# Delta-rule attention and an MLP on one core: a token group's key transposes are issued one unit earlier, and the last two output tiles leave with one DMA per queue instead of two

## The chip, the cores and the metric

One core of a Trainium2 chip runs the whole program. The metric is the device time of one execution in microseconds. Three runs of the kernel before took 662.1, 662.82 and 663.01 us; the median is 662.82 us.

## The reference

Two stages follow each other. The first is a delta-rule recurrence over 768 time steps for 4 batches and 8 heads of width 48. The second is an MLP with a hard-swish over 3072 tokens, with 384 inputs, 2048 hidden units and 384 outputs.

```python
q, k, v: (4, 8, 768, 48)   beta: (4, 8, 768)   w_in: (384, 2048)   w_out: (2048, 384)
k_n = k / (norm(k) + 1e-6);  state = 0                    # (B, H, 48, 48)
for t in range(768):
    y[t]   = q[t] @ state
    state += beta[t] * outer(k_n[t], v[t] - k_n[t] @ state)
x = y.transpose(0, 2, 1, 3).reshape(4 * 768, 8 * 48)      # row b*768 + s
h = x @ w_in
out = (h * clip(h + 3, 0, 6) / 6) @ w_out                 # (3072, 384), float32
```

A row of `out` is one token; the 768 tokens of a batch lie behind one another, so the same time steps of two batches lie 768 rows apart.

## The kernel before

**Tiles.** The 768 steps are cut into N = 24 chunks `t` of C = 32 steps. A chunk of all four batches fills the 128 partitions: batch b has the 32 partitions `rows(b)`. For every chunk there is a preparation, which does not need the state, and a chain, which does. Two chunks make a block (CB = 2) of 256 tokens, and the MLP works block by block: an "up" stage into the hidden units and a "down" stage out of them. There are 12 blocks, 0 to 11.

**Preparation** (`prep`, from L494). Its steps, one per `yield`: POOL normalises the keys into `kb` (L499); TensorE transposes the keys, four 128x128 transposes into a PSUM tile `pt` (L513), and ScalarE copies them to `KQ` (L521), after which POOL makes the mask `mb` (L475); TensorE transposes the queries and ScalarE copies them; TensorE multiplies the two into `sc` (L536); VectorE masks `sc` (L547).

**Chain** (`chain`, from L776). Products with the state `ks` (L795), VectorE combines them with the values to `R` (L890, L898), TensorE applies the inverse, `pz` (L816), ScalarE copies it back to `R` (L916), TensorE updates the state, `su` (L927, added on VectorE at L945), and the output part makes `y` (L832, L808, `py` L816, L852), transposes it, `yt` (L862), and ScalarE writes the transposed tile to the block's `xT` (L866), the MLP's input.

**MLP.** From block 3 on, "up" is `up_by_eleven` (L1055 products, ScalarE L1069, POOL sums L1019, VectorE L1082 and L1086). It multiplies sums of the four tiles of `xT`, which VectorE forms in `token_sums` (L1045) as soon as the block's second `xT` is there. From block 2 on, "down" is `down_by_seven` (L1215 products of 128x192, ScalarE copies L1222, POOL or VectorE adds L1225, VectorE sums L1201). The last adds finish the two output tiles `o[:, 0]` and `o[:, 1]`, and `to_dram` (L1140) stores them.

**What sets the order.** The program is written out by hand. An order string covers the beginning. Then a loop over the chunks (t from LS = 5 to 23) runs NU = 15 units per chunk; in each unit it takes steps of the chain and of the preparations by the table `plan`, then one step of the MLP (`take(units)`). Every engine executes its instructions in the order in which they were issued, so a step's place in `plan` decides what stands ahead of it on TensorE. For t = 6 and later, the preparation taken in `plan` (`now = third`) is that of chunk t + 6, so these steps exist for t = 6 to 17 (chunks 12 to 23). Its first step, `kb`, is taken in unit 13 of the chunk before (`later`). PSUM tiles of the MLP, the transposes, `pz`, `py` and `yt` share four banks (`pm`); a new tile takes the bank whose reader was issued longest ago.

**The output's rows.** `py` is written with the batches exchanged in pairs (`b ^ 1`), so the rows of x, and of `o`, carry batch b in the partitions of batch b ^ 1. `to_dram` undoes that with one DMA of 32 rows per batch. All stores go to SyncE's queue (SP), but for the last block (chunks 22 and 23), where batches 1 and 3 go to ScalarE's queue. In the last block chunk 22's tile leaves in two halves of 192 columns, the first half early; the others at the very end.

Of the kernel before, what the change touches and what calls it, by code (L numbers as in the profile page):

```python
# [14 lines left out]
ACTF = mybir.ActivationFunctionType  # L15
# [29 lines left out]
def kernel(  # L45
# [21 lines left out]
    nc = tc.nc  # L67
    B, H, S, D = q.shape
    DM, FF = moe_w_in.shape
    C, DP = 32, 64  # L70
    P = B * C
    assert P == 128 and S % C == 0 and D <= DP and H % 2 == 0
    N = S // C
# [6 lines left out]
    CB = 2  # L80
# [14 lines left out]
    def rows(b):  # L95
        return slice(C * b, C * b + C)
# [4 lines left out]
    def group(t):  # L101
        return (0, t) if t < G0 else ((t - G0) // GS + 1, (t - G0) % GS)
# [34 lines left out]
    def needs(*what):  # L137
        assert past.issuperset(what), (what, set(what) - past)
# [5 lines left out]
    def ring(tag, n, key):  # L144

        held = rings.setdefault(tag, [])
        i = len(held)
        if i < n:
            held.append(key)
        else:  # L150
            i = min(range(n), key=lambda i: reads.get(held[i], len(reads)))
            needs(("read", held[i]))
            held[i] = key
        slot[tag] = f"{tag}{i}"

    def read(*keys):
        for key in keys:
            past.add(("read", key))
            reads.setdefault(key, len(reads))
# [49 lines left out]
    for j, value in enumerate((1.0, -1.0)):  # L209
        m = mask2[:, j, :]  # L210
        for b in range(B):
            nc.gpsimd.memset(mask2[rows(b), j, :], value)
            nc.gpsimd.affine_select(
                out=mask2[rows(b), j, :], in_=mask2[rows(b), j, :], pattern=[[1, C]],
# [89 lines left out]
    for i, n in enumerate((0, 1, 2, 3, 4, 5, 0, 1, 3, 4, 5, 0, 1, 5, 0, 1)):  # L304
        s, f = weights[i][0].shape[1:]
# [458 lines left out]
    xTs, outs, zs = {}, {}, {}  # L764
# [5 lines left out]
    def he(h):  # L770
        return (h % 2) * NP + h // 2

    def by_pair(t):
        return t.rearrange("p (a e w) -> p e a w", e=2, w=D)

    def chain(t, whole=True):  # L776
# [29 lines left out]
        def plus(out, ph, sign, into):  # L806
            for e in range(2):
                nc.vector.scalar_tensor_tensor(  # L808
                    out=by_pair(out)[:, e], in0=ph[:, e], scalar=sign, in1=by_pair(into)[:, e],
                    op0=ALU.mult, op1=ALU.add,  # L810
                )
# [14 lines left out]
        def output(Z=None):  # L826

            if t > 0:
                needs(("turned", t - 1))
            y = work.tile([P, DM], FP32, name="y", bufs=1)  # L830
            if t > 0:
                nc.scalar.activation(  # L832
                    out=by_pair(y[:]), in_=even, func=ACTF.Copy, scale=parity[:, 1, 1:2]
                )
                past.add(("even", t))
                if ("R", t) in past:
                    read(("ks", t, 0))
                yield 1
                plus(y[:], odd, parity[:, 0, 1:2], y[:])
                read(*(("ks", t, i) for i in range(2)))  # L840
                yield
            needs(("Z", t))
            Z = zs.pop(t)
            ring("pm", NPM, ("py", t))
            py = psM.tile([P, 512], FP32, name="py", tag=slot["pm"])
            of_heads(py, lambda b: b ^ 1, lambda h: LB[:, he(h), :], Z)
            past.add(("BZ", t))
            yield
            if t == 0:
                nc.scalar.activation(out=y[:], in_=py[:, 0:DM], func=ACTF.Copy)  # L850
            else:
                nc.vector.tensor_tensor(out=y[:], in0=y[:], in1=py[:, 0:DM], op=ALU.add)  # L852
            read(("py", t))
            yield
            blk, cc = divmod(t, CB)
            if cc == 0:
                needs(*([("up", blk - 2)] if blk >= 2 else []))
                xTs[blk] = work.tile([128, NKT, TB], FP32, name="xT")
            ring("pm", NPM, ("yt", t))
            pt = psM.tile([128, NKT, P], FP32, name="yt", tag=slot["pm"])  # L860
            for s in range(NKT):
                nc.tensor.transpose(pt[:, s, :], y[:, s * 128 : (s + 1) * 128], ident[:])  # L862
            past.add(("turned", t))
            yield 1
            read(("yt", t))
            nc.scalar.activation(  # L866
                out=xTs[blk][:, :, cc * P : (cc + 1) * P], in_=pt[:], func=ACTF.Copy
            )
            past.add(("seam", t))
            yield  # L870

# [11 lines left out]
        else:  # L883
# [5 lines left out]
            for e in range(2):  # L889
                nc.vector.scalar_tensor_tensor(  # L890
                    out=Rp[:, e].rearrange("p (a w) -> p a w", w=D), in0=even[:, e],
# [4 lines left out]
            if whole:  # L896
                yield
            nc.vector.scalar_tensor_tensor(  # L898
                out=Rp, in0=odd.rearrange("p e a w -> p e (a w)"), scalar=parity[:, 1, 0:1],
# [43 lines left out]
        for i, x in enumerate(su):  # L943
            sv = state[:, 2 * i : 2 * i + 2].rearrange("p b a w -> p b (a w)")
            nc.vector.tensor_tensor(  # L945
                out=sv, in0=sv, in1=x[:, :, 0 : NP * D], op=ALU.subtract
# [187 lines left out]
                yield  # L1134

    def to_dram(t, o, m=slice(0, DM)):
        for b in range(B):
            r0 = b * S + t * C
            eng = nc.scalar if t >= N - CB and b % 2 else nc.sync
            eng.dma_start(out=out[r0 : r0 + C, m], in_=o[rows(b ^ 1), m])  # L1140

    def down(blk, c, f0):

# [186 lines left out]
    def take(gen, n=1):  # L1330
        for _ in range(n):
            while next(gen, None) == 1:
                pass
# [107 lines left out]
    with tc.manual_schedule():  # L1441
        for word in ORDER.split():
            word, _, n = word.partition("*")
            for _ in range(int(n or 1)):
                do(word)
        for name in relus:
            settle(0, name)
        while evicts:
            evicts.pop(0)()

        units = gens["u"]
        fill = inverse_of(2)
        loads = iter(())
        left = due = 0
        USED = {"up": 0.42, "eleven": 1.0, "down": 0.7}
        APART = (8, 12)
        CHAIN = {0: 0.45, 1: 0.75, 2: 0.75, 3: 0.4, 4: 0.4, 6: 0.5, 9: 0.8, 10: 0.6, 14: 0.2}
        for t in range(LS, N):
            g, i = group(t)
            ch = chain_of(t)  # L1460
            behind = t == LS
            now, more, third, later = (prep_of(t + LA - n) for n in (2, 1, 0, -1))
            if not behind:
                now = third
            take(gens["v"], 4)
            if i == 0:
                left += 1
            if i == 2:
                loads = keys_of(g + 3)
            plan = {  # L1470
                0: lambda: take(ch),
                1: lambda: (take(ch), take(now)),
                2: lambda: (take(ch), take(now), take(gens["q"], 4)),
                3: lambda: take(ch),
                4: lambda: (take(ch), take(now, t not in APART)),
                5: lambda: take(now, t not in APART),
                6: lambda: take(now),
                7: lambda: take(now, t in APART),
                8: lambda: take(ch),
                9: lambda: take(ch),  # L1480
                10: lambda: take(ch),
                11: lambda: token_sums(t // CB),
                13: lambda: take(later),
            }
            if behind:
                plan[13] = None
                for u, gen in zip((3, 5, 5, 6, 7, 9, 10, 11, 12, 13), (more,) * 5 + (third,) * 5):
                    plan[u] = lambda old=plan.get(u), gen=gen: (old and old(), take(gen))
            ready = (1, 6)
            for u in range(NU):  # L1490
                if plan.get(u):
                    plan[u]()
                take(loads, 2)
                if (i, u) == (0, 2):
                    drain(fill)
                    left = 0
                    fill = norms_of(g + 2)
                if (i, u) == ready:
                    drain(fill)
                    fill = inverse_of(g + 1)  # L1500
                    take(fill)
                    left, due = 2 * (C - 2) + 2, 0.0
                take(rest)
                take(gens["a"])
                take(units)
                settle(1)
                while evicts:
                    evicts.pop(0)()
                if i == 1 == ready[0] and 5 < u < 7:
                    continue  # L1510
                if i == 0 or not left:
                    take(fill, 2 if i or u < 2 else u > 4)
                    continue
                room = max(1.65 - USED[mode["of"]] - CHAIN.get(u, 0), 0.15) / mode["mean"]
                due += room * left / max((GS - i) * NU - u, 1)
                due = min(due, 2.6)
                take(fill, int(due))
                left, due = max(left - int(due), 0), due - int(due)
            if behind:
                take(later)  # L1520
            drain(ch)
        for _ in units:
            settle(2)
# [30 lines left out]
```

## Time and profile before

| what | value |
|---|---|
| median of three runs | 662.82 us |
| the profiled execution's own time | 662.71 us |
| its span from first to last instruction | 661.0 us |
| TensorE busy, share of the span | 96% |
| weight loads busy | 86% |
| VectorE / ScalarE / POOL busy | 76% / 40% / 34% |
| granted TensorE clock, mean | 0.99 |
| stores of output: 48 KB on SP / 24 KB on SP / 24 KB on ScalarE / 48 KB on ScalarE | 90 / 4 / 4 / 2 |

How to read it: a row of the timeline gives the start and the length in us, the engine, the line, the operation with its tiles and the number of instructions that were merged into the row. The length of a matmul is modelled and runs past the start of the next; what one costs is read from start to start. A float32 product has two records (the 32 products `ks` appear as x64), a transpose one. Engines with a `q` behind their name (SPq, ACTq, POOLq) are the sequencers, which issue DMAs and wait on semaphores. In a row of the windows view stand the stretch and its length, busy time and count of each engine, the clock, the mean busy share of the 16 DMA engines and the rate.

### The profile page before, as it was taken

What the parts mean: (1) busy time and instruction counts of PE and PEld (TensorE: products, weight loads), DVE (VectorE), ACT (ScalarE), POOL (GpSimd) and SP (SyncE); (2) the same over time, 40 slices, a digit from 0 to 9 for tenths busy, and PEclk for the clock granted to TensorE, in tenths of its full rate; (3) what the DMA queues carried; (4) which work ended last, traced back from release to release, by engine and by line L of the source; (5) the groups of instructions that cost most, each with busy time, mean ns of one, the idle gap of its engine ahead of it and who ended that gap; (6) DMA issues with size and microseconds to landing.
All of it is one profiled execution on the core that took longest, in us unless ns stands there. A gap on an engine that the chain in (4) does not pass through costs nothing.

```text
span 661.0 us, 26631 instructions
## 1 busy us (share of the span) xinstructions
PE 632.6 (96%) x11640; PEld 568.8 (86%) x11640; DVE 499.5 (76%) x1164; ACT 263.2 (40%) x547; POOL 226.6 (34%) x352
## 2 busy tenths in 40 slices
PE   2768999999999999999999999999999999999997
PEld 2658987776689989999999999999999999999997
DVE  5899877798657988758988748979658998456354
ACT  4786578322232154154144244244244144153240
POOL 5531023003661354453254354164152241331330
PEclk9979999999999999999999999999999999999999
DMA  7888246212041030041030030030020020000101
GB/s 171 210 216 217 76 100 165 49 25 39 16 84 20 2 75 3 3 83 28 3 74 3 2 74 3 2 63 2 3 50 2 2 49 3 23 18 2 26 1 24
DMA packets 88692, 33.28 MB, mean 50 GB/s; under 512 B 80224, under 2 KB 83424, under 8 KB 88576
## 3 DMA queue, kind: packets, MB, share of 16 engines
q1 hardware_dynamic: 88224, 31.29, 21.5%
q8 instruction: 91, 1.49, 0.9%
q10 hardware_dynamic: 352, 0.30, 0.2%
q14 instruction: 25, 0.20, 0.1%
HBM read 26.84 MB, written 4.72 MB: 48 GB/s over the span
## 4 chain that ended last, share of the span: by engine, by line
PE 91%; DVE 3%; DMA 2%; ACT 2%; SPq 1%; issue 1%; ACTq 0%; DVEq 0%
PE po L1215 28%; PE ph L1055 27%; PE ph L983 9%; PE po L1151 6%; PE ks L795 4%; PE pz L816 3%; PE pt L513 3%; PE py L816 3%; PE su L927 3%; PE sc L536 3%; ACT spare L345 1%; PE yt L862 1%; DMA w_out<-in_moe_w_in_dram 1%; SPq L168 1%; PE pi L673 1%
## 5 line engine op out<-in xcount | busy, mean ns | idle before, releaser
L1055 PE MATMUL ph<-xT,w_in 128*128 128x128 f32 (+1 forms) x720 | 156.7, 321 | 0.2 <-issue 0.2
L1019 POOL TENSOR_TENSOR g<-g 128x256 f32<-128x256 f32 (+1 forms) x144 | 88.0, 612 | 105.5 <-ACT g L1069 99.9
L1055 PEld LDWEIGHTS ph<-xT,w_in 128*128 128x128 f32 x720 | 116.9, 191 | 6.7
L1215 PE MATMUL po<-w_out,g 128*128 128x192 f32 x640 | 110.6, 326 | 0.0
L1215 PEld LDWEIGHTS po<-w_out,g 128*128 128x128 f32 x640 | 104.6, 190 | 0.5
L1215 PE MATMUL po<-spare,g 128*128 128x192 f32 x480 | 86.7, 332 | 0.0
L1069 ACT ACTIVATE g<-ph 128x512 f32<-128x512 f32 x72 | 43.0, 597 | 107.5 <-PE ph L1055 107.5
L1215 PEld LDWEIGHTS po<-spare,g 128*128 128x128 f32 x480 | 77.2, 190 | 1.8
L983 PE MATMUL ph<-xT,w_in 128*128 128x128 f32 (+1 forms) x384 | 72.8, 339 | 1.5 <-ACT xT L866 0.6
L1225 POOL TENSOR_TENSOR o<-o,u 128x192 f32<-128x192 f32 x18 | 14.9, 828 | 163.5 <-ACT o L1222 76.1
L983 PEld LDWEIGHTS ph<-xT,w_in 128*128 128x128 f32 x384 | 60.2, 196 | 9.0 <-DVE g L993 0.9
L1082 DVE TENSOR_TENSOR g<-ph,g 128x256 f32<-128x256 f32 x72 | 30.2, 419 | 47.3 <-PE ph L1055 44.8
L748 DVE TENSOR_TENSOR pr<-A 128x30 f32<-128x30 f32 (+9 forms) x150 | 57.6, 384 | 3.3
L1201 DVE TENSOR_TENSOR g<-g 128x512 f32<-128x512 f32 x80 | 55.3, 712 | 3.6 <-PE po L1215 3.6
L1102 DVE SCALAR_TENSOR_TENSOR g<-o,g 128x512 f32<-128x512 f32 x72 | 52.5, 729 | 7.2 <-ACT o L1099 7.2
L753 DVE TENSOR_TENSOR A<-A,pr 128x30 f32<-128x30 f32 (+9 forms) x150 | 55.1, 367 | 3.3
L1055 PE MATMUL ph<-beta_tok,sums_in 128*128 128x128 f32 x288 | 55.9, 275 | 0.1
L1099 ACT ACTIVATE o<-g 128x512 f32<-128x512 f32 x72 | 45.4, 631 | 12.0 <-DVE g L1102 8.5
L345 ACT ACTIVATE spare<-spare 128x768 uint16<-128x768 uint16 (+1 forms) x56 | 47.3, 850 | 3.2 <-DMA kf<-in_k_dram 1.7
L499 POOL TENSOR_TENSOR kb<-kf,inv 128x384 f32<-128x384 f32 x24 | 21.7, 906 | 75.5 <-issue 42.6
L1222 ACT ACTIVATE o<-po 128x192 f32<-128x192 f32 x40 | 13.2, 330 | 83.2 <-PE po L1215 83.2
L1151 PE MATMUL po<-w_out,g 128*128 128x384 f32 x128 | 45.4, 490 | 0.0
(137 smaller groups left out, 1010.2 us busy)
## 6 DMA issues: line engine op xcount, KB each, us to landing
kf<-in_k_dram SPq DMA_DIRECT2D x96, 48.0 KB, 3.0
qb<-in_q_dram SPq DMA_DIRECT2D x96, 48.0 KB, 2.6
vf<-in_v_dram SPq DMA_DIRECT2D x96, 48.0 KB, 2.5
out_dram<-o SPq DMA_DIRECT2D x90, 48.0 KB, 1.6
spare<-in_moe_w_in_dram SPq DMA_DIRECT2D x4, 768.0 KB, 5.3
w_out<-in_moe_w_in_dram SPq DMA_DIRECT2D x4, 768.0 KB, 5.6
w_out<-in_moe_w_out_dram SPq DMA_DIRECT2D x4, 768.0 KB, 7.0
spare<-in_moe_w_out_dram SPq DMA_DIRECT2D x4, 768.0 KB, 4.9
```

Of the source, the lines that this page charges most:

```text
L345: nc.scalar.activation(out=z, in_=z if n else d.bitcast(I16)[:, :, :, 3], func=func, bias=value, scale=scale,)
L748: nc.vector.tensor_tensor(out=pv, in0=A[:, j + 1 :, j].unsqueeze(2).to_broadcast([n, w, j]), in1=A[:, j, 0:j].unsqueeze(1).to_broadcast([n ...
L753: nc.vector.tensor_tensor(out=A[:, j + 1 :, 0:j], in0=A[:, j + 1 :, 0:j], in1=pv, op=ALU.subtract)
L983: nc.tensor.matmul(ph[:, cols], lhsT=w_in[:, s, f * 128 : (f + 1) * 128], rhs=xT[:, s, cols], start=(s == 0), stop=(s == NKT - 1),)
L1019: nc.gpsimd.tensor_tensor(out=out, in0=a, in1=b, op=op)
L1055: nc.tensor.matmul(ph[:, n], lhsT=w, rhs=x, start=start, stop=stop, skip_group_check=True)
L1069: nc.scalar.activation(out=gt, in_=ph[:], func=ACTF.Copy)
L1099: nc.scalar.activation(out=r, in_=g, func=ACTF.Relu, bias=0.5, scale=1.0 / 6.0)
L1102: nc.vector.scalar_tensor_tensor(out=g, in0=r, scalar=1.0, in1=g, op0=ALU.min, op1=ALU.mult)
L1151: nc.tensor.matmul(pos[c][:], lhsT=gs[blk, f // 2][:, f % 2, c * P : (c + 1) * P], rhs=w_out[:, f, :], start=(f == 0), stop=(f == NFC - 1),)
L1201: nc.vector.tensor_tensor(out=A(f, *out, 4), in0=A(f, *a, 4), in1=A(f, *b, 4), op=op)
L1215: nc.tensor.matmul(ps[n][:], lhsT=A(f - f % 2, *a)[:, f % 2], rhs=b[:, f], start=(f == 0), stop=(f == HF - 1),)
```

## The change

```diff
@@ chain, output part
-            nc.scalar.activation(
-                out=xTs[blk][:, :, cc * P : (cc + 1) * P], in_=pt[:], func=ACTF.Copy
-            )
+            xt = xTs[blk][:, :, cc * P : (cc + 1) * P]
+            if blk + 1 < N // CB:
+                nc.scalar.activation(out=xt, in_=pt[:], func=ACTF.Copy)
+            else:
+                xt, src = (x.rearrange("p s (i j c) -> j p s i c", j=2, c=C) for x in (xt, pt[:]))
+                for j in range(2):
+                    nc.scalar.activation(out=xt[j], in_=src[1 - j], func=ACTF.Copy)
@@ to_dram
+        if t >= N - CB:
+            by_batch = out.rearrange("(b s) m -> b s m", s=S)[:, t * C : (t + 1) * C, m]
+            half = B // 2
+            for i, eng in enumerate((nc.sync, nc.scalar)):
+                eng.dma_start(
+                    out=by_batch[i * half : (i + 1) * half],
+                    in_=o[i * half * C : (i + 1) * half * C, m],
+                )
+            return
         for b in range(B):
             r0 = b * S + t * C
-            eng = nc.scalar if t >= N - CB and b % 2 else nc.sync
-            eng.dma_start(out=out[r0 : r0 + C, m], in_=o[rows(b ^ 1), m])
+            nc.sync.dma_start(out=out[r0 : r0 + C, m], in_=o[rows(b ^ 1), m])
@@ the loop over the chunks
+            if not behind:
+                plan.update({
+                    0: lambda: (take(ch), take(now)),
+                    1: lambda: take(ch),
+                })
```

Three things change. First, for t = 6 to 17 the keys' transposes move from unit 1 to unit 0: on TensorE they stand directly behind the products `ks`, and the MLP's step of unit 0 comes after them. Their copy on ScalarE moves ahead of one MLP copy, and in the blocks with `up_by_eleven` the mask on POOL moves ahead of one pair of sums. Second, in the last block x is written with the batches back in their own places, in two ScalarE operations of 192 elements per partition instead of one of 384. Third, therefore, a tile of the last block is stored with one DMA on each queue: 64 partitions of `o`, read as 64 rows, written to a pattern of 2 batches by 32 rows by 192 or 384 columns. Before, each queue had two DMAs of 32 rows by 32 rows. The last block's three stores make 6 DMAs instead of 12. VectorE's order, and SP's ahead of the last block, stay as they were.

## The prediction

> **What bounds the kernel now.** I read the page first: the busy times and the chain that ended last.
>
> ```profile
> span 661.0 us, 26631 instructions
> ...
> PE 632.6 (96%) x11640; PEld 568.8 (86%) x11640; DVE 499.5 (76%) x1164; ACT 263.2 (40%) x547; POOL 226.6 (34%) x352
> ...
> PE 91%; DVE 3%; DMA 2%; ACT 2%; SPq 1%; issue 1%; ACTq 0%; DVEq 0%
> ```
>
> TensorE holds 91% of the chain. After the start it hardly waits, so time can be won on it only through fewer or cheaper records, and at the end of the program only through what follows its last product. The timeline of the last microseconds and the windows behind it show that part.
>
> ```profile
> 656.87 1.92 SPq L1140 DMA_DIRECT2D out_dram<-o  x4
> 656.87 1.93 ACTq L1140 DMA_DIRECT2D out_dram<-o  x4
> 657.57 0.35 DVE L1225 TENSOR_TENSOR o<-u,po 128x192 f32<-128x192 f32 x1 [0.73 <-PE po L1215]
> ```
>
> ```profile
> 656.80:657.60 0.80, 0.73 (x5) 0.43 (x3) 0.07 (x2) 0.00 (x0) 0.00 (x0) 1.00 0.00 0
> 657.60:657.80 0.20, 0.00 (x0) 0.00 (x0) 0.20 (x1) 0.00 (x0) 0.00 (x0) 1.00 0.40 100
> 657.80:658.60 0.80, 0.00 (x0) 0.00 (x0) 0.12 (x1) 0.00 (x0) 0.00 (x0) 1.00 0.90 213
> 659.20:659.60 0.40, 0.00 (x0) 0.00 (x0) 0.00 (x0) 0.00 (x0) 0.00 (x0) 1.00 0.51 117
> 659.60:659.80 0.20, 0.00 (x0) 0.00 (x0) 0.00 (x0) 0.00 (x0) 0.00 (x0) 1.00 0.05 12
> 659.80:661.00 1.20, 0.00 (x0) 0.00 (x0) 0.00 (x0) 0.00 (x0) 0.00 (x0) 0.59 0.00 0
> ```
>
> The last two columns are the DMA engines' mean busy share and the rate in GB/s. The stores of chunk 23 are issued at 656.87. The first bytes move at about 657.7, 0.8 us later. The last add ends at 657.92 and releases the second half of chunk 22. The last bytes move at about 659.7, and the span ends 1.3 us after them. From 657.92 on nothing but stores is left: every microsecond that they take longer is a microsecond of the result.
>
> **The transposes.** They are moved, not removed; the step issues the four transposes, one ScalarE copy and the mask, and no DMA. Twelve chunks have them (t = 6 to 17). I price them by TensorE's timeline, start to start, first at t = 9 and then at t = 5, where the trace already has transposes directly behind `ks`.
>
> ```profile
> 258.80 1.15 PE L795 MATMUL ks<-state,KQ 64*64 64x48 f32 x64
> 259.88 1.57 PE L1215 MATMUL po<-spare,g 128*128 128x192 f32 x8
> 261.29 0.60 PE L513 MATMUL pt<-ident,kb 128*128 128x128 f32 x4
> 261.72 1.47 PE L1215 MATMUL po<-spare,g 128*128 128x192 f32 x8
> 263.03 0.60 PE L513 MATMUL pt<-ident,qb 128*128 128x128 f32 x4
> ```
>
> ```profile
> 117.75 0.66 PE L513 MATMUL pt<-ident,kb 128*128 128x128 f32 x4
> ...
> 118.24 0.60 PE L513 MATMUL pt<-ident,qb 128*128 128x128 f32 x4
> ...
> 118.68 1.13 PE L1151 MATMUL po<-w_out,g 128*128 128x384 f32 x3
> ```
>
> Eight `po` records cost 1.41 us behind `ks` and 1.31 behind transposes: coming from the small tiles costs them 0.10. Four transposes cost 0.49 behind `ks` and 0.44 behind other transposes: 0.05. Today the 0.10 is paid, afterwards the 0.05, since the MLP then comes behind transposes. That is 12 x 0.05 = 0.6 us won. The `up_by_eleven` chunks pay the same entry:
>
> ```profile
> 234.88 0.49 PE L1055 MATMUL ph<-xT,w_in 128*128 128x128 f32 x2
> 235.21 0.39 PE L1055 MATMUL ph<-beta_tok,sums_in 128*128 128x128 f32 x2
> ...
> 235.88 0.60 PE L513 MATMUL pt<-ident,kb 128*128 128x128 f32 x4
> ```
>
> The first pair takes 0.33, the other three 0.67 together, 0.22 each: 0.11 for the entry. The bounds of the gain are 0 (all entries alike) and 12 x 0.10 = 1.2 us (transposes enter free).
>
> What the moved step needs must be ready about 1.0 to 1.4 us earlier. Its keys are tightest in these chunks:
>
> ```profile
> 233.57 0.98 POOL L499 TENSOR_TENSOR kb<-kf,inv 128x384 f32<-128x384 f32 x1
> ...
> 237.97 1.19 POOL L475 TENSOR_TENSOR mb<-beta_tok,mask 128x256 f32<-128x256 f32 x2
> ```
>
> ```profile
> 241.97 0.41 DVE L1082 TENSOR_TENSOR g<-ph,g 128x256 f32<-128x256 f32 x1
> ```
>
> `kb` ends at 234.55, 0.33 us ahead of the products' end at 234.88, so I cost the wait at nothing; without that cover it is a rival below. The mask, 1.19 us, now stands ahead of the POOL sums of the third product group. They can come later by that much at most; their reader on VectorE runs at 241.97, some 4 us after them. The ScalarE copy `KQ` (0.6 us) goes ahead of one copy whose bank is next needed a unit later. For the transposes' bank, in the odd chunks the one that `po` took at 259.88 goes to them at the same time. Nothing queues behind any of this that TensorE needs sooner.
>
> **x in two operations.**
>
> ```profile
> L866 ACT ACTIVATE xT<-yt 128x384 f32<-128x384 f32 x24 | 11.8, 490 | 46.1 <-PE yt L862 46.0
> L1222 ACT ACTIVATE o<-po 128x192 f32<-128x192 f32 x40 | 13.2, 330 | 83.2 <-PE po L1215 83.2
> ```
>
> ```profile
> 618.87 0.68 DVE L1045 TENSOR_TENSOR xT<-xT 128x128 f32<-128x128 f32 x1
> ...
> 619.46 0.28 DVE L1045 TENSOR_TENSOR beta_tok<-xT,beta_tok 128x128 f32<-128x128 f32 x1
> ...
> 620.14 0.39 PE L1055 MATMUL ph<-xT,w_in 128*128 128x128 f32 x2
> ```
>
> Two ScalarE operations of 192 elements take 0.66 us instead of 0.49: 0.17 later; if each cost as much as the whole, 0.49 later. VectorE's sums follow. The third, ending at 619.55, is needed at 620.14: 0.59 of slack. I take nothing, and above 0.59 the excess would count.
>
> **The stores.** Two DMAs per queue become one, so the second issue of the last pair falls away: 0.36 us, the distance between two issues on SP (363 ns median below). But the shape changes too, and the DMA views show what hangs on it.
>
> ```profile
> L1140 SPq DMA_DIRECT2D out_dram<-o x6: 314/363/479, 647.9 to 658.3; - x6
> ```
>
> ```profile
> DMA packets 576, 0.39 MB, mean 23 GB/s; under 512 B 192, under 2 KB 576, under 8 KB 576
> ```
>
> ```profile
> q10 hardware_dynamic: 64, 0.10, 7.1%
> ...
> spare<-in_beta_dram ACTq DMA_DIRECT2D x4, 24.0 KB
> ```
>
> The first DMA row is of 645 to 662 us: 12 stores of 32 rows. The rows are 768 or 1536 bytes, so the 192 small packets are something else, 16 per store: one completion per DMA engine. The second is of the first 7.5 us: four loads of `beta` on ScalarE's queue, 8 rows of 3072 bytes each. Of their 64 packets 32 are rows, which leaves 8 completions per load. So 32 outer rows ran on 16 engines and 8 outer rows on 8: a DMA is cut along its outermost count. The new stores have 64 outermost in SBUF and **2** outermost in DRAM. All transfers of this trace have the same outer count on both sides, so it does not say which side decides; a cut has to fall in the same place on both, and the smaller count allows 2. The bounds are 2 engines and 16, and I take 2. Whether both queues get the same two is not shown either: 2 or 4 engines together. I take 2, since both queues spread over the same 16 today.
>
> The Trainium skill says the same ("DMA: Bandwidth & Descriptors", section "Why a DMA increments its semaphore by 16 and not by 1"): a DMA runs on the largest number of engines up to 16 that divides the slowest dimension of both sides, which is 2 here, and on these queues on the lowest-numbered ones, so the same two. The 16 and the 8 above agree; no run here shows a 2 yet.
>
> What an engine moves, from the busiest stretch of the loads:
>
> ```profile
> 40.00:41.50 1.50, 1.50 (x9) 1.50 (x8) 1.50 (x4) 1.44 (x3) 0.83 (x1) 0.50 0.99 371
> ```
>
> 371 GB/s over 16 x 0.99 busy engines is 23.4 GB/s for one; in the stores above, 213 over 16 x 0.90 is 14.8, with all engines reading the same 32 partitions at once. Behind the end stand 4 x 48 KB and 4 x 24 KB = 288 KB = 295 kB. Two engines need 295 / 46.8 = 6.3 us, or at 14.8 each 10.0 us. I take 6.3, because two engines crowd each other less than sixteen. The issue of the new form is not shown: nothing more at best, 0.2 at worst (the longest store issue, 479 ns, less 314); I take 0.1. The last bytes then move at 657.7 + 0.1 + 6.3 = 664.1 instead of 659.7: **4.4 us later**. The early half of chunk 22's store, 10 us ahead, is hidden even so.
>
> The Trainium skill's figure of about 27 GiB/s per engine (same page, section "Specifications") would give, as an estimate, 5.1 us instead of 6.3.
>
> **The sum.** The profiled execution took 662.71 us, 0.11 under the median. 662.71 - 0.6 + 4.4 = **666.5 us**, 0.6% slower.
>
> **The rivals.**
> - *The stores keep 16 engines* (SBUF's 64 rows decide). Not slower: the last issue falls away, 662.71 - 0.6 - 0.36 = 661.75. The point of decision: with n engines the bytes end at 657.7 + 12.6 / n, which equals 659.7 + 0.6 at n = 5. For it speaks that 64 rows are there to be cut, against it the 8 of the `beta` loads. Chance 0.10.
> - *Two engines per queue, four in all*: 3.15 us, 657.7 + 0.1 + 3.15 = 660.95, so 662.71 + 1.25 - 0.6 = 663.4. Nothing in the rows speaks for it. Chance 0.05.
> - *Two engines at the crowded rate*: 10.0 us, 662.71 + 8.1 - 0.6 = 670.2. For it speaks that 14.8 is the rate of stores, against it that sixteen shared one group of partitions. Chance 0.20.
> - *The transposes wait for `kb`*: from a lateness of 0.33 us on, in the five `up_by_eleven` chunks. If `kb` began only at the products' end, 0.98 x 5 = 4.9 us on top, 671.4. Against it speaks that POOL's work ahead of `kb` is not changed. Chance 0.03.
>
> **How the numbers follow.** The forecast has 0.62. Its own range comes from the DMA view of 8 to 50 us, 40 slices:
>
> ```profile
> DMA  7699999999999799773799938997457999277999
> GB/s 120 121 390 312 229 310 372 230 124 318 363 161 125 162 362 301 138 127 65 140 394 305 182 74 153 369 301 150 75 89 224 390 237 125 39 111 172 384 326 393
> ```
>
> The fastest slice moves 394 GB/s at a digit of 9, so at most 27 GB/s per engine, 5.4 us; with 1.2 won on the transposes and no longer issue, 662.71 + 3.4 - 1.2 = 664.9. Above, it meets the crowded rate. I give 664.9 to 670.4, which holds the forecast and the third rival. A measurement of this kernel tells about 0.2% (1.3 us) from no change: slower 0.85 (forecast and the last two rivals), the same 0.13, faster 0.02 (the first rival with all 1.2 us won).
>
> **What would show it.** In the changed kernel the DMA share behind 658 us should be near 2/16 = 0.13 for some 6 us, at about 47 GB/s, and the 6 stores should leave 12 small packets instead of 192. TensorE's last product should end 0.6 us earlier, with `pt` 0.49 us behind `ks` and `po` at 1.31 per eight records after it, and no wait on `kb`. If the share behind 658 is again 0.5 to 0.9, the first rival holds and the forecast is wrong.

## The result, and the profile after

The changed kernel took 668.93 us (median of 6 runs, 668.21 to 669.08), beside 662.46 us (660.83 to 665.27) for the kernel before in the same rounds. The ratio is 1.0087, with a 95% interval of 1.0067 to 1.0108: slower by 4.4 to 7.2 us. The forecast was 666.5 us, with a range of 664.9 to 670.4.

The page of the changed kernel, with the span, the busy times and the chain that ended last:

```profile
span 666.9 us, 26608 instructions
...
PE 631.7 (95%) x11640; PEld 568.1 (85%) x11640; DVE 501.7 (75%) x1164; ACT 265.0 (40%) x549; POOL 227.4 (34%) x352
...
PE 91%; DMA 3%; DVE 3%; issue 1%; SPq 1%; ACT 1%; DVEq 0%
```

TensorE's busy time fell by 0.9 us, and yet the span grew by 5.9. The end of the program shows where. First the timeline (start, length, engine, line, operation), then the windows behind it (stretch and length, busy time of PE, PEld, DVE, ACT and POOL, clock, DMA share, GB/s), then the count of packets from the DMA view of 648 to 668 us:

```profile
656.96 1.60 ACTq L1145 DMA_DIRECT2D out_dram<-o  x2
657.66 0.35 DVE L1237 TENSOR_TENSOR o<-u,po 128x192 f32<-128x192 f32 x1 [0.73 <-PE po L1227]
```

```profile
657.60:658.00 0.40, 0.02 (x1) 0.00 (x0) 0.34 (x1) 0.00 (x0) 0.00 (x0) 1.00 0.00 0
658.00:659.40 1.40, 0.00 (x0) 0.00 (x0) 0.01 (x1) 0.00 (x0) 0.00 (x0) 1.00 0.12 16
659.40:662.00 2.60, 0.00 (x0) 0.00 (x0) 0.00 (x0) 0.00 (x0) 0.00 (x0) 1.00 0.13 40
662.00:665.00 3.00, 0.00 (x0) 0.00 (x0) 0.00 (x0) 0.00 (x0) 0.00 (x0) 0.64 0.13 47
665.00:665.60 0.60, 0.00 (x0) 0.00 (x0) 0.00 (x0) 0.00 (x0) 0.00 (x0) 0.50 0.13 42
665.60:666.90 1.30, 0.00 (x0) 0.00 (x0) 0.00 (x0) 0.00 (x0) 0.00 (x0) 0.50 0.00 1
```

```profile
DMA packets 396, 0.39 MB, mean 20 GB/s; under 512 B 12, under 2 KB 396, under 8 KB 396
```

The last add ends at 657.66 + 0.35 = 658.01, and the span goes on to 666.9: 8.9 us with nothing in them but stores, where the kernel before had 3.1 (657.92 to 661.0). The DMA share there is 0.13, which is 2 of 16 engines, all the time, and the six stores leave 12 small packets, 2 each. The share before was up to 0.90, with 16 small packets per store. The rate is 16 GB/s in the first 1.4 us and comes up to 47.

On TensorE the products `ks` of t = 6 and t = 18 frame the twelve chunks in which the transposes moved. Their rows, first of the kernel before, then of the changed one:

```profile
183.17 1.15 PE L795 MATMUL ks<-state,KQ 64*64 64x48 f32 x64
...
484.31 1.15 PE L795 MATMUL ks<-state,KQ 64*64 64x48 f32 x64
```

```profile
184.33 1.15 PE L795 MATMUL ks<-state,KQ 64*64 64x48 f32 x64
...
484.41 1.15 PE L795 MATMUL ks<-state,KQ 64*64 64x48 f32 x64
```

With these rows and the last adds both spans fall into four parts:

| part | before | after | difference | forecast |
|---|---|---|---|---|
| start to `ks` of t = 6 | 183.17 | 184.33 | +1.16 | 0 |
| `ks` of t = 6 to `ks` of t = 18 | 301.14 | 300.08 | -1.06 | -0.6 |
| `ks` of t = 18 to the end of the last add | 173.61 | 173.60 | 0.0 | 0 |
| end of the last add to the end of the span | 3.1 | 8.9 | +5.8 | +4.4 |
| span | 661.0 | 666.9 | +5.9 | +3.8 |

The first part has the same instructions in both kernels. Over these two and the seven other profiled executions below, its end lies anywhere from 180.9 to 186.6 us, so the +1.16 is scatter of single executions. The other three parts agree between executions of the same code within 0.15 us. Together they say +4.8 us, inside the measured 4.4 to 7.2.

### The profile page after: what moved, and what is told of

It reads as the page before. It is cut to its first block, busy times and chain, and to the rows that moved or that the text cites. A ratio compares the mean times of both kernels' runs of the same rounds, so it can differ in the third digit from the quotient of the medians.

```text
span 666.9 us, 26608 instructions
## 1 busy us (share of the span) xinstructions
PE 631.7 (95%) x11640; PEld 568.1 (85%) x11640; DVE 501.7 (75%) x1164; ACT 265.0 (40%) x549; POOL 227.4 (34%) x352
## 4 chain that ended last, share of the span: by engine, by line
PE 91%; DMA 3%; DVE 3%; issue 1%; SPq 1%; ACT 1%; DVEq 0%
PE po L1227 28%; PE ph L1059 27%; PE ph L987 9%; PE po L1163 6%; PE ks L795 4%; PE pt L513 4%; PE su L931 3%; PE pz L816 3%; PE py L816 3%; PE sc L536 3%; PE yt L862 1%; DMA w_out<-in_moe_w_in_dram 1%; PE pi L673 1%; DMA spare<-in_moe_w_in_dram 1%; DMA qb<-in_q_dram 1%
## 5 line engine op out<-in xcount | busy, mean ns | idle before, releaser
L1227 PE MATMUL po<-spare,g 128*128 128x192 f32 x480 | 85.1, 331 | 0.0
L1237 POOL TENSOR_TENSOR o<-o,u 128x192 f32<-128x192 f32 x18 | 13.4, 744 | 163.2 <-ACT o L1234 75.5
```

What stands on the lines that cost most here:

```text
L1227: nc.tensor.matmul(ps[n][:], lhsT=A(f - f % 2, *a)[:, f % 2], rhs=b[:, f], start=(f == 0), stop=(f == HF - 1),)
```

## The experiments

The theory is that of the prediction: the time went to the six new stores, because the 2 that stands outermost in their DRAM pattern lets each use two DMA engines, and the move of the transposes gives back a little. The rivals to be told apart from it: the two-level pattern, or the smaller number of DMAs, is slow by itself however many engines there are; and the transposes or the split of x cost something that the tail hides. The first four of them (stores of 32 rows to four engines) were timed beside a kernel before of 663.05 us (median, 29 runs), the last three beside one of 661.52 us (17 runs); the last two have a single run and are read from their traces. The small packets in the table are the completions, one per engine and store.

| kernel | ratio to before, 95% interval | `ks` t = 6 to t = 18 | last add to end | small packets |
|---|---|---|---|---|
| before | 1 | 301.14 | 3.1 | 192 |
| changed | 1.0087 (1.0067 to 1.0108) | 300.08 | 8.9 | 12 |
| stores of 32 rows | 0.9993 (0.9979 to 1.0007) | 300.10 | 3.1 | 192 |
| stores alone | 1.0093 (1.0071 to 1.0115) | 301.02 | 8.9 | 12 |
| transposes alone | 0.9988 (0.9972 to 1.0004) | 300.08 | 3.0 | 192 |
| four engines | 1.0014 (1.0000 to 1.0028) | 300.06 | 5.0 | 24 |
| steps outermost | 1.0002 (0.9986 to 1.0019) | 300.07 | 3.2 | 96 |
| one queue | one run, 669.87 us | 300.08 | 8.9 | 12 |
| last half only | one run, 661.71 us | 300.06 | 5.3 | 132 |

### Stores of 32 rows: the change with the old stores

```diff
-            for i, eng in enumerate((nc.sync, nc.scalar)):
-                eng.dma_start(out=by_batch[i * half : (i + 1) * half], in_=o[i * half * C : (i + 1) * half * C, m])
+            for b in range(B):
+                r0 = b * S + t * C
+                eng = nc.scalar if b % 2 else nc.sync
+                eng.dma_start(out=out[r0 : r0 + C, m], in_=o[rows(b), m])
```

> The changed kernel with the last block's stores cut into 32 rows again, two DMAs per queue; x in two operations and the moved transposes stay. If the stores' two DMA engines are the whole loss: 661.9 us, 0.6 under the kernel before, 192 small packets behind 645 us, span end some 3.1 us after the last add begins its wait. If the moved transposes or the two-part x cost time (a wait that the profiled run hides): over 662.5, up to 668.9.

The timeline and the windows of this kernel, in which the transposes are moved and x is written in two operations:

```profile
659.96 0.35 DVE L1234 TENSOR_TENSOR o<-u,po 128x192 f32<-128x192 f32 x1 [0.73 <-PE po L1224]
```

```profile
660.20:661.00 0.80, 0.00 (x0) 0.00 (x0) 0.11 (x1) 0.00 (x0) 0.00 (x0) 1.00 0.88 210
661.00:662.20 1.20, 0.00 (x0) 0.00 (x0) 0.00 (x0) 0.00 (x0) 0.00 (x0) 1.00 0.37 87
662.20:663.50 1.30, 0.00 (x0) 0.00 (x0) 0.00 (x0) 0.00 (x0) 0.00 (x0) 1.00 0.00 0
```

With the old stores the DMA share is again 0.88 and the tail (from the end of the last add to the end of the span) again 3.1 us (660.31 to 663.4). All of the +5.8 hangs on the form of the six stores. The whole time is 662.57 us beside 663.05 for the kernel before: 0.5 less where 0.6 was expected, but with its interval not to be told from no change. It lies just above the 662.5 that was named as the sign of a cost, but the kernel before took 0.6 us longer in these rounds than in those of the result, so it does not show one. The part between `ks` of t = 18 and the last add, in which x is split, did not change either, so the split costs nothing.

### Stores alone: the transposes back in their place

```diff
-            if not behind:
-                plan.update({
-                    0: lambda: (take(ch), take(now)),
-                    1: lambda: take(ch),
-                })
```

> The changed kernel with the transposes back in unit 1; the two-part x and the one store per queue stay. If the stores are the loss and the transposes a gain of 0.6: 669.5 us, and the same 12 small packets behind 645 us. If the transposes are part of the loss: under 668.9.

Its `ks` of t = 6 and t = 18, and the windows behind its last add, which ends at 659.17:

```profile
184.55 1.15 PE L795 MATMUL ks<-state,KQ 64*64 64x48 f32 x64
...
485.57 1.15 PE L795 MATMUL ks<-state,KQ 64*64 64x48 f32 x64
```

```profile
659.20:660.40 1.20, 0.00 (x0) 0.00 (x0) 0.00 (x0) 0.00 (x0) 0.00 (x0) 1.00 0.11 14
...
662.40:666.80 4.40, 0.00 (x0) 0.00 (x0) 0.00 (x0) 0.00 (x0) 0.00 (x0) 0.58 0.13 46
```

The whole loss is there without the moved transposes, with the same slow first 1.2 us, and the gain on TensorE is gone: 301.02, as before. Its 670.09 us are 7.0 over the kernel before in the same rounds, as expected (669.5 over 662.5). The two parts of the change add up.

### Transposes alone: the kernel before with the new plan

```diff
+            if not behind:
+                plan.update({
+                    0: lambda: (take(ch), take(now)),
+                    1: lambda: take(ch),
+                })
```

> The kernel before with the transposes alone moved. If entering the large tiles from ks costs 0.05 less each time: 661.9 us, TensorE 12 x 0.05 = 0.6 shorter between 184 and 485 us, no wait for kb. If kb or a bank holds them up: 662.5 to 665.

Its page's first line and the two `ks`:

```profile
span 658.8 us, 26613 instructions
```

```profile
182.15 1.15 PE L795 MATMUL ks<-state,KQ 64*64 64x48 f32 x64
...
482.23 1.15 PE L795 MATMUL ks<-state,KQ 64*64 64x48 f32 x64
```

Between the two it needs 300.08 us, 1.06 less than before. The gain is real in every profiled execution with the new plan (300.06 to 300.10 in seven kernels, against 301.14 and 301.02 with the old one). In whole times it is too small to be told from nothing: 0.9988, and the interval reaches 1.0004. Of the 2.2 us by which its span is shorter, 1.0 is scatter of the start.

### Four engines: the same number of DMAs, four outermost

Each queue takes half of the columns of all four batches. A store then reads 128 rows of `o` and writes 4 batches by 32 rows.

```diff
-            for i, eng in enumerate((nc.sync, nc.scalar)):
-                eng.dma_start(out=by_batch[i * half : (i + 1) * half], in_=o[i * half * C : (i + 1) * half * C, m])
+            half = (m.stop - m.start) // 2
+            for i, eng in enumerate((nc.sync, nc.scalar)):
+                w = slice(m.start + i * half, m.start + i * half + half)
+                eng.dma_start(out=by_batch[:, t * C : (t + 1) * C, w], in_=o[:, w])
```

> The changed kernel with its last stores cut by columns instead of batches: each queue stores half of the columns of all four batches, 4 by 32 rows of 128 partitions, so still one DMA per queue, but 4 outermost in DRAM. If the outermost count sets the number of engines: 4 engines, 24 small packets behind 645 us, 3.1 us of bytes instead of 6.3, so about 665.8 us. If the loss is a fixed cost of DMAs with two levels of rows: 668.9. If each queue uses engines of its own: 8 busy engines and 664.2.

Its DMA view of 645 to 672 us:

```profile
GB/s 0 0 0 0 0 0 0 49 24 0 70 3 0 0 0 0 0 0 0 25 89 63 88 83 78 12 0 0 0 0 12 0 0 0 0 0 0 0 0 0
DMA packets 793, 0.40 MB, mean 15 GB/s; under 512 B 536, under 2 KB 792, under 8 KB 792
```

512 of the 536 small packets are rows of 96 columns (384 bytes); 24 are left, 4 per store. The rate goes up to 89 GB/s, about twice that of the changed kernel, and the tail falls from 8.9 to 5.0 us. As the columns differ, SP's store of chunk 23 could also be issued 0.66 us ahead of ScalarE's, so the tail is not a pure count of engines. The whole time, 664.93 us, is 0.9 under the 665.8 expected for four engines and 0.7 over the 664.2 for eight, so it does not tell the two apart. The share does: from 660.0 to 662.2, where both queues move bytes (222 packets and 132), it is 0.25, four of 16. Two engines became four with the 2 that became 4.

### Steps outermost: 16 engines with one DMA per queue

This kernel tells the count of engines from the form. ScalarE writes x of the last block with the two batches of a half alternating, so that the partitions of `o` hold step 0 of both batches, step 1 of both, and so on. The DRAM pattern is then 32 steps by 2 batches instead of 2 batches by 32 steps. The number of DMAs, their 64 partitions and their bytes stay as in the change.

```diff
-                xt, src = (x.rearrange("p s (i j c) -> j p s i c", j=2, c=C) for x in (xt, pt[:]))
+                src = pt[:].rearrange("p s (i j c) -> j p s i c", j=2, c=C)
+                xt = xt.rearrange("p s (i c j) -> j p s i c", j=2, c=C)
...
-            by_batch = out.rearrange("(b s) m -> b s m", s=S)[:, t * C : (t + 1) * C, m]
+            by_step = out.rearrange("(i j s) m -> i s j m", i=half, s=S)[:, t * C : (t + 1) * C, :, m]
...
-                eng.dma_start(out=by_batch[i * half : (i + 1) * half], in_=o[i * half * C : (i + 1) * half * C, m])
+                eng.dma_start(out=by_step[i], in_=o[i * half * C : (i + 1) * half * C, m])
```

> The changed kernel with the last block's tokens laid out step by step: ScalarE writes x with the two batches of a half alternating (a stride of two elements), so that each store's DRAM pattern is 32 steps by 2 batches instead of 2 batches by 32 steps. Still one DMA per queue and tile, 64 partitions and the same bytes. If the smaller outermost count decides how many engines a store gets, 32 gives 16 engines: 96 small packets (6 x 16), a DMA share of 0.4 to 0.9 behind 657.7, and from the last add to the end of the span 2.7 to 3.1 us as with stores of 32 rows (3.1), less the second issue of 0.36; ratio to the kernel before 0.997 to 1.000. If a store of 64 partitions with a two-level DRAM pattern, or one DMA per queue, is slow in itself, 12 small packets and 8.9 us from the last add to the end remain, ratio 1.009.

Its windows behind the last add (657.69 + 0.35 = 658.04), its DMA view of 645 to 672 us, and the durations of its issues (least, median, most, in ns):

```profile
658.00:658.80 0.80, 0.00 (x0) 0.00 (x0) 0.04 (x1) 0.00 (x0) 0.00 (x0) 1.00 0.71 171
658.80:659.60 0.80, 0.00 (x0) 0.00 (x0) 0.00 (x0) 0.00 (x0) 0.00 (x0) 1.00 0.54 147
...
660.00:661.20 1.20, 0.00 (x0) 0.00 (x0) 0.00 (x0) 0.00 (x0) 0.00 (x0) 0.98 0.00 0
```

```profile
DMA packets 481, 0.40 MB, mean 15 GB/s; under 512 B 96, under 2 KB 480, under 8 KB 480
```

```profile
L1146 SPq DMA_DIRECT2D out_dram<-o x3: 534/541/655, 648.0 to 658.1; - x3
L1146 ACTq DMA_DIRECT2D out_dram<-o x3: 553/567/638, 649.9 to 658.1; - x3
```

96 small packets are 16 per store, the share is 0.71 and the tail 3.2 us. Six DMAs of 64 partitions with a two-level pattern are not slow; a 2 in front of the pattern is. At best 0.36 us less was expected from the issue that falls away, and it did not come: the tail is just outside the 2.7 to 3.1 expected. One issue of this form takes 0.54 to 0.57 us where one of 32 rows took 0.36 to 0.40, and the first byte comes 1.19 us behind the beginning of the issue (658.18 behind 656.99) instead of 0.81. The bytes themselves took 1.7 us (to 659.90) instead of 2.0, so the later first byte costs more than they win. So the idea behind the change, one store per queue, brings nothing measurable even with all 16 engines (1.0002, with the moved transposes in it).

### One queue: both stores of chunk 23 on SP

```diff
-            for i, eng in enumerate((nc.sync, nc.scalar)):
+            for i, eng in enumerate((nc.sync, nc.sync if t == N - 1 else nc.scalar)):
```

> The changed kernel with both stores of chunk 23 on SP, one behind the other; only chunk 22's last half still has its second store on ScalarE's queue. In the changed kernel the first 1.3 us of the last stores run at 16 GB/s instead of 47, which costs about 0.9 us. If that comes from two queues starting on the same two engines at the same time, the full 47 GB/s are there within 0.5 us of the first byte and the bytes end some 0.9 us earlier: 8.0 us from the last add to the end of the span. If every such store begins slowly, or the packets of the first store do, it stays at 8.7 to 9.1.

Its windows from the last add (658.62) on:

```profile
658.70:659.90 1.20, 0.00 (x0) 0.00 (x0) 0.00 (x0) 0.00 (x0) 0.00 (x0) 1.00 0.12 17
659.90:662.00 2.10, 0.00 (x0) 0.00 (x0) 0.00 (x0) 0.00 (x0) 0.00 (x0) 1.00 0.13 40
662.00:666.20 4.20, 0.00 (x0) 0.00 (x0) 0.00 (x0) 0.00 (x0) 0.00 (x0) 0.55 0.13 45
```

The slow start is there as before, 17 GB/s for 1.2 us, with only one queue at work, and the tail stays 8.9. My explanation of it, two queues that start on the same two engines at once, fell. The trace of the changed kernel speaks against it as well: all 40 packets between 658.0 and 660.5 belong to SP's queue, so ScalarE's store moved nothing yet while the rate was low.

### Last half only: one merged pair of stores at the very end

Chunk 23 and the early half of chunk 22 keep DMAs of 32 rows.

```diff
+            if t == N - 1 or m.start == 0:
+                for b in range(B):
+                    r0 = b * S + t * C
+                    eng = nc.scalar if b % 2 else nc.sync
+                    eng.dma_start(out=out[r0 : r0 + C, m], in_=o[rows(b), m])
+                return
```

> The changed kernel with chunk 23 and the early half of chunk 22 stored as four DMAs of 32 rows each; only the last half of chunk 22 (98 kB) leaves as one DMA per queue. If two engines at 46.8 GB/s are the whole price, the bytes take 2.1 us from about 1.2 us behind the last add on, and 4.6 us lie between the last add and the end of the span. If the slow start of 0.9 us comes with every pair of such stores, 5.5. If the size of a store were not what counts but the form itself, 8.9 as in the changed kernel.

Its windows behind the last add (654.26 + 0.35 = 654.61):

```profile
654.90:655.50 0.60, 0.00 (x0) 0.00 (x0) 0.00 (x0) 0.00 (x0) 0.00 (x0) 1.00 0.62 146
655.50:655.80 0.30, 0.00 (x0) 0.00 (x0) 0.00 (x0) 0.00 (x0) 0.00 (x0) 1.00 0.00 0
655.80:656.50 0.70, 0.00 (x0) 0.00 (x0) 0.00 (x0) 0.00 (x0) 0.00 (x0) 1.00 0.11 24
656.50:658.60 2.10, 0.00 (x0) 0.00 (x0) 0.00 (x0) 0.00 (x0) 0.00 (x0) 0.86 0.13 39
658.60:660.00 1.40, 0.00 (x0) 0.00 (x0) 0.00 (x0) 0.00 (x0) 0.00 (x0) 0.50 0.00 0
```

Here one sees both forms behind each other: the old stores of chunk 23 at a share of 0.62 until 655.5, then a pause until the merged pair begins, then 98 kB on two engines, 2.8 us long instead of the 2.1 that 46.8 GB/s would give. The tail is 5.3 us, 2.2 more than with stores of 32 rows. The price grows with the bytes behind the end: 2.2 us for 98 kB, 5.8 for 295 kB. A slow start comes with this pair too, but a smaller one: 0.7 x (46.8 - 24) / 46.8 = 0.3 us.

## Why the prediction was right, and where its sizes were off

**What bounds the kernel.** Right. The gain on TensorE and the loss behind the last add went into the span in full, and nothing between them moved.

**The count of engines.** Right, and this decided the sign. The prediction could not see a 2 in the trace and reasoned from 32 rows on 16 engines and 8 rows on 8. The runs complete the row: 2 gave 2 (12 small packets from 6 stores), 4 gave 4 (24), 32 in front of the same 64 partitions gave 16 (96). All these counts are powers of two, so the runs do not tell the smaller count from the largest common divisor. That both queues have the same two engines is in the share, 0.13 and not 0.25, while both move bytes. The queues of the changed kernel from 662 to 665 us (packets, MB, share of 16 engines; q10 is ScalarE's, q1 SP's):

```profile
q10 hardware_dynamic: 77, 0.09, 8.4%
q1 hardware_dynamic: 64, 0.05, 4.7%
```

The Trainium skill's rule ("DMA: Bandwidth & Descriptors", section "Why a DMA increments its semaphore by 16 and not by 1"), the largest number up to 16 that divides the slowest dimension of both sides, agrees with all three; its lowest-numbered engines agree with the 0.13. The first rival (16 engines) and the second (four in all) fell.

**The rate of the two engines.** The steady rate was right: 47 GB/s against the 46.8 that were taken from the loads. The rival of the crowded rate, 14.8 GB/s per engine, fell: sixteen engines again moved 171 / (16 x 0.71) = 15 each in the kernel with the steps outermost, two moved 23.5. But the term of 6.3 us was too small: the bytes took 7.6 us, from 658.1 to 665.7. In the first 1.4 us only 16 GB/s moved, which loses 1.4 x (46.8 - 16) / 46.8 = 0.9 us, and in the next 2.6 us 40, another 0.4. I had taken one rate for the whole transfer; no row of before showed a transfer of so few engines from its first byte on. The DMA view of 658.0 to 659.2 shows where the slow start lies:

```profile
DMA packets 12, 0.02 MB, mean 15 GB/s; under 512 B 0, under 2 KB 12, under 8 KB 12
...
q1 hardware_dynamic: 12, 0.02, 12.7%
```

The two engines are busy all the while: 12 rows of 1536 bytes took 0.127 x 16 x 1.2 = 2.4 us of engine time, 0.20 us each, where 23.5 GB/s makes it 0.065. Each row itself takes three times as long at first. Why is not shown.

The Trainium skill's figure of about 27 GiB/s per engine ("DMA: Bandwidth & Descriptors", section "Specifications"), which is 29 GB/s, with its estimate of 5.1 us, lies farther off: the trace has 23.5 GB/s per engine at its steadiest.

**Issue and first byte.** I took 0.1 for the new form's issue. The issues and what follows them:

```profile
L1145 SPq DMA_DIRECT2D out_dram<-o x3: 512/526/677, 648.0 to 658.0; - x3
L1145 ACTq DMA_DIRECT2D out_dram<-o x3: 522/522/649, 649.9 to 658.0; - x3
```

An issue took 0.52 us instead of 0.36 on SP and 0.40 on ScalarE, and the first byte came at 658.1, 1.15 us after the beginning of the issue at 656.96 instead of 0.81: 0.34 later, where I had taken 0.1 and 0.2 at worst. The issue got longer by 0.16 on SP, whose bytes came first; that is about half of it. Together, 0.34 for the first byte, 7.6 - 2.0 = 5.6 for the bytes, and 0.1 less between the last bytes and the end of the span (1.2 instead of 1.3) give the 5.8 that were measured for the 4.4 of the forecast.

**The transposes.** The mechanism was right. The chunk t = 9 of the changed kernel:

```profile
259.81 1.15 PE L795 MATMUL ks<-state,KQ 64*64 64x48 f32 x64
260.89 0.66 PE L513 MATMUL pt<-ident,kb 128*128 128x128 f32 x4
261.38 2.77 PE L1227 MATMUL po<-spare,g 128*128 128x192 f32 x16
263.99 0.27 PE L513 MATMUL pt<-ident,qb 128*128 128x128 f32 x1
```

`pt` takes 0.49 behind `ks`, and 16 records of `po` take 2.61, 1.305 per eight: both as forecast. From `ks` to the queries' transposes it is 4.18 us instead of 4.23. Twelve times 0.05 is 0.6; the measured gain is 1.06. From one `ks` to the next, ten of the twelve chunks are 0.04 to 0.06 us shorter than in the kernel before, t = 14 is 0.19 shorter and t = 16 is 0.39 shorter. So the 0.6 is there, chunk by chunk, and the rest lies in two places. One is in the chunk t = 16, in the kernel before:

```profile
443.05 0.39 PE L1055 MATMUL ph<-xT,w_in 128*128 128x128 f32 x2
443.27 0.74 PE L1055 MATMUL ph<-beta_tok,sums_in 128*128 128x128 f32 x2
443.85 0.39 PE L1055 MATMUL ph<-xT,w_in 128*128 128x128 f32 x2
```

One pair of these products follows another after 0.22 us; here it is 0.58, with no releaser named: 0.36 more. The same pause, 0.38 us long, stands at the same pair in the kernel with the stores alone, and not in the changed kernel, which needs 0.22 there. What it waits for the trace doesn't show, so its cause stays open; that both kernels with the old plan have it is all that the runs show. The other is in t = 14, 24.94 us long before and 24.75 after. The kernel with the stores alone, which has the old plan, needs 24.80 there, so 0.14 of it belong to that one execution and not to the plan. That the bound of 1.2 us was nearly reached is therefore no sign that the transposes enter free.

`kb` made no product wait in these chunks: the only wait of `pt` for `kb` in the changed kernel is one of 8.1 us, ahead of the moved steps. The fourth rival fell.

**x in two operations.** Its price of nothing was right. The two take 0.55 us together (0.17 more was the estimate, 0.06 came):

```profile
617.38 0.55 ACT L872 ACTIVATE xT<-yt 128x192 f32<-128x192 f32 x2 [3.61 <-PE yt L862]
...
618.96 0.68 DVE L1049 TENSOR_TENSOR xT<-xT 128x128 f32<-128x128 f32 x1
...
620.23 0.39 PE L1059 MATMUL ph<-xT,w_in 128*128 128x128 f32 x2
```

The third sum ends at 619.64 and is needed at 620.23: the same 0.59 of slack as before.

**The sum.** The two errors pull in opposite directions: the stores cost 1.4 us more than forecast, and the transposes' part gave 0.46 more, which hides a third of that by luck. With these sizes the prediction's working would have read 662.71 - 1.06 + 5.8 = 667.5 us, against 668.93 measured. The +4.8 that they add lies within the measured 4.4 to 7.2; the rest of the median's distance, 1.4 us, is less than what the start alone varies by.

## What to carry to other kernels

Before two stores are merged into one, look at the outermost count of both patterns: a DMA used as many engines as the smaller count allowed (2, 4 or 16 here), and a transfer that nothing hides then takes longer for it (7.6 us on two engines instead of 2.0 on sixteen). If a merged store is wanted, bring a long dimension to the front on the DRAM side, which here took only another order of the tokens in a copy that was made anyway. And price the merge itself first: here the merged form's longer issue and later first byte left nothing of the issue that was saved.

## What the runs showed of the hardware that was not expected

- A store on two engines starts slowly: 14 to 17 GB/s in the first 1.2 to 1.4 us of three kernels, 24 GB/s for 0.7 us when the rows were 768 bytes, then up to 47. In all of them only SP's queue moved bytes in that stretch. The issue doesn't set the pace: the same bytes to 16 engines ran at 171 GB/s in their first 0.8 us, and on two engines the rows themselves took 0.20 us each instead of 0.065 while the engines were busy. What makes them slow was not found.
- An issue with a two-level DRAM pattern took 0.52 to 0.57 us (median) on SP and ScalarE in the changed kernel (64 rows), the one with four engines (128 rows) and the one with the steps outermost (64 rows); one of 32 plain rows took 0.36 to 0.40. The first byte of chunk 23 came 1.15 to 1.19 us behind the beginning of the issue instead of 0.81.
- The start of the program, up to `ks` of t = 6, took 180.9 to 186.6 us in nine profiled executions of the same instructions. Comparing the parts behind it resolved 0.15 us where whole times resolve a microsecond.
